# Independent scatters, a spread narrowing of two matrices, and a reordered first cycle in a filter, routing and expert kernel

## The chip, the core and the metric

The kernel runs on one core of a Trainium2 chip. Five engines work side by side: PE multiplies matrices (PEld loads its weights), ACT applies functions and casts, DVE and POOL do elementwise work, POOL also issues indirect DMAs, and SP issues the other DMAs. The metric is the device time of one execution in microseconds (us), the median of several.

## What is computed

Three layers in a row, all results in fp32:

```
X  = rfft(x, axis=1)                    # x: 4 x 3072 x 256
Y  = shrink(X @ (w_r + i w_i) + b)      # sign(.) * max(|.| - 0.01, 0), real and imaginary part
a  = irfft(Y).reshape(12288, 256)
e  = argmax(a @ w_gate); g = softmax weight of e
y  = g * (relu(a @ w1[e]) @ w2[e])      # 8 experts, the first 384 tokens of each; others give 0
h  = y @ w_in; out = (h * sigmoid(h)) @ w_out   # 256 -> 2048 -> 256
```

w_in and w_out arrive as float64.

## The kernel before

The Fourier transforms are products with tables (`first`, `s1`, `kphase`, `is2`, `third`). As 8 experts take 384 tokens each, only batch 0 and the first 1,024 tokens of batch 1 are computed (`near`); a branch at the end (L1269), on a flag that tells whether all experts are full, holds the rest and is not taken here. Tokens of a layer that no expert takes are zeros, written by `zero_out` on SP.

Every fp32 product is made of three matmuls (`mm3`, L205 to L207) on a high and a low part; `split` makes them, the high part by a cast on ACT (L189), the low part by a subtraction on DVE or POOL (L197). The float64 matrices are read as pairs of int32 and brought to fp32 by `narrow` (an absolute value on ACT, four operations on DVE, L868 to L874) and then split: `ffn_in` handles w_in in eight chunks, and forms on POOL the four sums s1 to s4 of its blocks (the `mixed` tensor); `ffn_out` handles w_out in eight chunks, a chunk at each of the steps that `AHEAD` names and at the first five steps of the first pair.

`experts` runs the order 0, 1, 2, E, 3, 4, E+1, 5, 6, E+2, 7, E+3. A number below E is one expert's own FFN (`first_ffn`: eight tiles hp of 128 x 384, rectified into hh on ACT and hl on DVE, which are consumed by the products y). E+q is the second FFN of a pair of experts (`second_ffn`): in each of eight cycles seven products h of a Winograd scheme, with the sums u (L1210) on DVE, Silu on ACT (L1151) and a split into gh and gl; m1 to m4, b2 and yT are the sums of the pair's inputs, made by `pair`. The three sums that come from `mixed` are loaded as mt and split into the tile ring, with the low part on POOL (`load`, `cut`). The products o with w_out of one cycle fill the next one; those of a pair's last cycle are closed in the first cycle of the next pair (`close`), evicted to the tile `tail` (L1182) and scattered to out by an indirect DMA of 128 rows (`scatter`, L1253). For the last pair the sums are finished at the end (L1241 to L1248), and the six scatters follow behind the branch (end of `body`). `gather` collects an expert's tokens by three indirect DMAs (L1040), `turn` transposes them (gtp) and, for expert 0, runs 12 matmuls on zeros behind (pw, L1063); `weights` loads an expert's weights as tiles st and splits them into w.

While experts 0 to 2 run, `beside` finishes the attention's second block and its routing: `third` (ps, ao, tp, lg, and lt, the transposed gate values, L602), `choose` (Exp on ACT), `route` (the counts bs, L695, and the tables tb, L753) and `slots`, which makes the positions of experts 3 to 7 with a temporary tmp of its own (L801).

A tile belongs to a ring of a few buffers (`bufs`), and its writer waits until the last reader of the buffer's earlier tile is done. The order on each engine is set by a list scheduler from the program's order and its dependencies; `after` adds an order between two instructions without a semaphore. Two scatters write the same tensor, so without more each waits for the one before.

Of the kernel before, what the change touches and what calls it, by code (L numbers as in the profile page):

```python
# [9 lines left out]
F32 = mybir.dt.float32  # L10
# [3 lines left out]
AF = mybir.ActivationFunctionType  # L14
# [9 lines left out]
P = 128  # L24
# [7 lines left out]
NF = 3  # L32
# [4 lines left out]
WARM = 11  # L37
AHEAD = 7, 15, 23
PMS = "vav"
# [114 lines left out]
class Kernel:  # L154
# [95 lines left out]
    def near(self):  # L250

        ads, self.bds, self.res = {}, {}, {}
        self.left = ExitStack()
        self.kp = self.left.enter_context(self.tc.tile_pool(name="kpa", bufs=2, reuse_waits="tile"))
        with self.stream("a", 3, "right"), self.sums("a", 2):
            self.warm()
            self.first()
            tables, spectra = self.load_tables(), self.kphase(0, ads)
            for g in (tables, spectra, tables, spectra, spectra):
                next(g)  # L260
            mix([tables, spectra, self.s1(1, ads), self.ffn_in()], [4, 10, 24, 15], lead=[0, 0, 0, 0])
            rest = self.kphase(1, ads, True)
            next(rest)
            with self.tc.issue_after(self.fetched):
                self.route_consts()
            mix([self.is2(0, (0, 1, 2), self.res)], [1])
            self.route(0, (0, 1, 2), self.res)
            self.rank()
            self.early = self.slots(self.cst, 0, EARLY, self.sel, "s")[0]
            for _ in rest:  # L270
                pass
# [271 lines left out]
    def choose(self, lt, out, gs):  # L543

        nc, v, bp = self.nc, self.nc.vector, self.bp
        oh, m2, sm = out
        sh = [P, lt.shape[1], gs.stop - gs.start, E]
        L = bp.tile(sh, F32, tag="L", name="L")
        mx = bp.tile(sh[:3] + [1], F32, tag="mx", name="mx")
        v.tensor_reduce(mx, lt, AX.X, ALU.max)  # L550
        sc = bp.tile(sh, F32, tag="sc", name="sc")
        v.tensor_tensor(sc, lt, mx.to_broadcast(sh), ALU.is_equal)
        v.tensor_tensor(L, lt, mx.to_broadcast(sh), ALU.subtract)
        nc.scalar.activation(L, L, AF.Exp)
        v.tensor_tensor(sc, sc, self.pri.to_broadcast(sh), ALU.mult)
        v.tensor_reduce(m2[:, :, gs], sc, AX.X, ALU.max)
        v.tensor_tensor(oh[:, :, :, gs].rearrange("p e b g -> p b g e"), sc, m2[:, :, gs].to_broadcast(sh), ALU.is_equal)
        v.tensor_reduce(sm[:, :, gs], L, AX.X, ALU.add)
# [230 lines left out]
    def slots(self, pool, s0, s1, sel, tag, work=None):  # L789
# [6 lines left out]
        if sel is None:  # L796
            v.tensor_copy(ent, T.rearrange("p x e -> p e x"))
        else:
            sh = [P, n, NF * SC, E]
            tmp = work.tile(sh, F32, name=f"tmp{tag}", bufs=1)  # L800
            v.tensor_tensor(tmp, T.rearrange("p (o x) e -> p o x e", o=1).to_broadcast(sh),  # L801
                            sel[:, s0:s1].rearrange("p s (o e) -> p s o e", o=1).to_broadcast(sh), ALU.mult)
            v.tensor_reduce(ent, tmp, AX.X, ALU.add)
# [81 lines left out]

    def ffn_in(self):

        W = 512
        nc, g = self.nc, self.nc.gpsimd
        for _ in range(LATE):  # L890
            yield
        for q in range(8):
            h, z = q % 2, (q // 2) * W
# [25 lines left out]
    def experts(self, again=False):  # L919
# [17 lines left out]
        def beside():  # L937

            with self.stream("b", 2, "left"):
                for n, _ in enumerate(self.third(1, self.res)):  # L940
                    yield 2 + 2 * n
                self.route(1, (0,), self.res)
                self.sl.extend(self.slots(self.mc, EARLY, E, self.sel, "t", self.bp)[0])
                self.filled()
            self.po, self.mb = pool("po", **ps), pool("mb")

        fw = self.ffn_out()
        if again:
            self.sl = self.compact(self.mc)
            self.po, self.mb = pool("po", **ps), pool("mb")  # L950
            side = iter(())
            for _ in self.ffn_in():
                pass
        else:
            self.sl = list(self.early)
            side = beside()
# [4 lines left out]
        xg = {e: self.gather(e) for e in order[:2]}  # L961
        xs[0] = self.turn(xg.pop(0), None if again else 12)
        ws = {e: self.weights(e, n) for e, n in zip(order[:2], (3, 4))}
# [3 lines left out]
        for at, ph in enumerate(order):  # L967
            if ph == E:
                for _ in side:
                    pass  # L970
                pre = self.pair()
            after = order[at + 1] if at + 1 < len(order) else E
            if after < E and after not in ws:
                xg[after] = self.gather(after)
                ws[after] = self.weights(after)
            part = self.first_ffn(ph, xs.pop(ph), ws[ph][0]) if ph < E else self.second_ffn(ph - E, pre)
            for m, _ in enumerate(part):
# [4 lines left out]
                while due is not None and due <= n:  # L982
                    due = next(side, None)
                if n in AHEAD or (ph == E and m < 5):
                    next(fw, None)
# [62 lines left out]
    def turn(self, rows, zeros=0, behind=None):  # L1048
# [11 lines left out]
        if zeros:  # L1060
            pw = self.pm.tile([P, 2 * D], F32, tag="y", name="pw")
            for n in range(zeros):
                self.after(self.nc.tensor.matmul(pw[:, :D], self.zr[:, :P], self.zr[:, :D], start=True, stop=True).ins, last.ins)  # L1063
        return xT

    def first_ffn(self, e, xT, ws):
# [5 lines left out]
        for j in range(NJ + 1):  # L1072
# [10 lines left out]
            if j > 0:  # L1083
                hh, hl = hs.pop(j - 1)
                for h in range(2):
                    w, c = w2[(j - 1) // 2], slice(h * P, (h + 1) * P)
                    self.mm3(yp[h], w[:, 0, (j - 1) % 2, c], w[:, 1, (j - 1) % 2, c], hh, hl, j == 1, j == NJ)
            yield
# [30 lines left out]
    def second_ffn(self, q, pre):  # L1119
# [58 lines left out]
        def close(us, s_):  # L1178
            for n, u in enumerate(us):
                second(u, s_, stop=n == len(us) - 1)  # L1180
            oo = rows(s_)
# [5 lines left out]
        load(1)  # L1187
        cut(0)
        for i in range(NI):
            load(i + 2)  # L1190
# [20 lines left out]

            for step in (1, 6, 0, 7, 4, 2, 0, 5, 3, 0) if final else (1, 0, 6, 2, 0, 7, 5, 0, 4, 3, 0):
                if step == 0:
# [5 lines left out]
                elif step == 2:  # L1219
                    add(u1, product(a12, b21), u1)  # L1220
                    self.unit[11] = gated(u1, "v", 2 * i, 0)
                elif step == 7:
                    add(u3, product(s3, m3), u2)
                elif step == 5:
# [3 lines left out]
                    add(u2, h, u2)  # L1228
                    self.unit[22] = gated(to, "p" if final else "v", 2 * i + 1, 1, "w0" if final else None)
                elif step == 4:  # L1230
# [21 lines left out]
    def scatter(self, oo, at, n):  # L1252
        self.nc.gpsimd.indirect_dma_start(  # L1253
            out=self.o["out"][0:n], out_offset=bass.IndirectOffsetOnAxis(ap=at, axis=0),
            in_=oo, in_offset=None, bounds_check=n - 1, oob_is_err=False)

# [47 lines left out]
```

## Time and profile before

| | us |
|---|---|
| median of 3 runs | 657.82 |
| lowest, highest | 654.78, 659.46 |
| the profiled execution | 659.92 |
| its span, first to last instruction | 658.1 |
| PE busy in it | 608.9 |

The rows further down come from that one profiled execution. Times count from the start of its span; L12 is line 12 of the kernel before. "out<-in" names the tiles an instruction writes and reads; what stands behind "<-" in brackets is what ended an engine's idle time.

### The profile page before, as it was taken

How to read it: one execution, taken by the hardware profiler on the slowest of the kernel's cores; microseconds unless marked ns; L12 is line 12 of the kernel's file. 1: busy time of each engine (PE TensorE's matmuls, PEld its weight loads, DVE VectorE, ACT ScalarE, POOL GpSimd, SP SyncE). 2: the span in 40 equal slices, each digit the busy share in tenths (PEclk: the TensorE clock that was granted, in tenths of full speed). 3: DMA queues.
4: the chain of work that ended last, by engine and by line, in shares of the span. 5: the costliest groups of instructions: out<-in, count | busy, mean ns of one | idle time of the engine just before them, and what ended most of it. 6: DMA issues, size and time to landing. Idle time of an engine off the chain costs nothing. (4 is left out here: it accounts for less than half of the span.)

```text
span 658.1 us, 11494 instructions
## 1 busy us (share of the span) xinstructions
PE 608.9 (93%) x4128; PEld 562.8 (86%) x4128; DVE 424.4 (64%) x832; ACT 339.7 (52%) x721; POOL 198.3 (30%) x201
## 2 busy tenths in 40 slices
PE   9999979999979989899999999999999999899940
PEld 8988769568967779799889999999999999799940
DVE  2447796355953659889987785577785574665630
ACT  2545554344533544566565675555665564565520
POOL 1004461000060001356663423453213443354312
PEclk9999999999998999879999999999999999999985
DMA  8547985965266766532434442323432300110000
GB/s 219 164 143 229 325 255 157 233 174 163 105 218 194 189 194 187 188 90 96 135 93 132 151 143 90 121 79 118 136 109 89 121 25 29 37 32 14 1 21 32
DMA packets 66010, 86.08 MB, mean 131 GB/s; under 512 B 6068, under 2 KB 55864, under 8 KB 65944
## 3 DMA queue, kind: packets, MB, share of 16 engines
q1 hardware_dynamic: 53976, 69.53, 34.9%
q10 hardware_dynamic: 9664, 9.44, 4.7%
q0 software_dynamic: 2304, 6.29, 2.9%
q8 instruction: 34, 0.56, 0.4%
q14 instruction: 32, 0.26, 0.2%
HBM read 54.31 MB, written 30.93 MB: 130 GB/s over the span
## 5 line engine op out<-in xcount | busy, mean ns | idle before, releaser
L1210 DVE TENSOR_TENSOR u<-h,u 128x384 f32<-128x384 f32 x224 | 117.3, 552 | 57.5 <-PE h L207 51.0
L1151 ACT ACTIVATE u<-u 128x384 f32<-128x384 f32 x128 | 64.6, 522 | 73.8 <-DVE u L1210 72.0
L206 PE MATMUL o<-wo,gl 128*128 128x256 f32 x369 | 100.2, 283 | 0.8 <-POOL gl L197 0.8
L207 PE MATMUL o<-wo,gh 128*128 128x256 f32 x369 | 99.9, 283 | 0.0
L205 PE MATMUL o<-wo,gh 128*128 128x256 f32 x369 | 87.3, 283 | 0.1
L197 POOL TENSOR_TENSOR gl<-u,gh 128x384 fp32r<-128x384 f32 x62 | 66.8, 1094 | 31.8 <-ACT gh L189 25.5
L197 POOL TENSOR_TENSOR ring<-mt,ring 128x384 fp32r<-128x384 f32 x32 | 37.5, 1173 | 119.9 <-ACT ring L189 118.3
L206 PEld LDWEIGHTS o<-wo,gl 128*128 128x128 f32 x369 | 70.0, 190 | 1.5 <-POOL gl L197 1.4
L207 PEld LDWEIGHTS o<-wo,gh 128*128 128x128 f32 x369 | 70.2, 190 | 0.0
L205 PEld LDWEIGHTS o<-wo,gh 128*128 128x128 f32 x369 | 65.6, 191 | 0.4 <-ACT gh L189 0.4
L189 ACT CAST gh<-u 128x384 fp32r<-128x384 f32 x126 | 63.6, 510 | 4.1 <-PE o L207 2.1
L197 DVE TENSOR_TENSOR w<-st,w 128x512 fp32r<-128x512 f32 x64 | 43.7, 694 | 25.2 <-ACT w L189 19.9
L1081 DVE SCALAR_TENSOR_TENSOR hl<-hp,hh 128x384 fp32r<-128x384 f32 x64 | 35.1, 553 | 36.1 <-ACT hh L1080 30.1
L205 PE MATMUL yp<-wri,xk 128*128 128x256 f32 x188 | 57.4, 305 | 0.4 <-ACT xk L454 0.4
L206 PE MATMUL yp<-wri,xk 128*128 128x256 f32 x188 | 54.8, 291 | 0.3 <-DVE xk L453 0.3
L207 PE MATMUL yp<-wri,xk 128*128 128x256 f32 x188 | 54.0, 287 | 0.0
L189 ACT CAST w<-st 128x512 fp32r<-128x512 f32 x64 | 38.8, 621 | 26.0 <-DMA st<-in_moe_w 15.8
L1080 ACT ACTIVATE hh<-hp 128x384 fp32r<-128x384 f32 x64 | 31.1, 490 | 37.2 <-PE hp L207 23.1
L205 PE MATMUL y<-hh,w 128*128 128x384 f32 x128 | 44.3, 346 | 3.2 <-ACT hh L1080 3.2
L205 PE MATMUL hp<-xT,w 128*128 128x384 f32 x128 | 44.2, 346 | 2.5 <-ACT w L189 2.5
L206 PE MATMUL hp<-xT,w 128*128 128x384 f32 x128 | 43.8, 343 | 0.1
L207 PE MATMUL hp<-xT,w 128*128 128x384 f32 x128 | 43.5, 341 | 0.0
(254 smaller groups left out, 1508.8 us busy)
## 6 DMA issues: line engine op xcount, KB each, us to landing
st<-in_moe_w SPq DMA_DIRECT2D x64, 256.0 KB
out<-zt SPq DMA_DIRECT2D x48, 256.0 KB
b_d<-bo ACTq DMA_DIRECT2D x12, 512.0 KB
mt<-mixed SPq DMA_DIRECT2D x32, 192.0 KB
xt<-in_x SPq DMA_DIRECT2D x15, 384.0 KB
nt<-in_moe_w_in SPq DMA_DIRECT2D x8, 512.0 KB
nt<-in_moe_w_out SPq DMA_DIRECT2D x16, 256.0 KB
a_d<-ao SPq DMA_DIRECT2D x8, 384.0 KB
```

The source lines that it names most:

```text
L189: self.lastact = self.nc.scalar.copy(dst, src)
L197: return e.tensor_tensor(dst, src, raw(hi), ALU.subtract).ins
L205: first = nc.tensor.matmul(out, lh, rh, start=start, stop=False)
L206: nc.tensor.matmul(out, ll, rh, start=False, stop=False)
L207: return first.ins, nc.tensor.matmul(out, lh, rl, start=False, stop=stop).ins
L1080: self.rectified = nc.scalar.activation(hh, hp, AF.Relu).ins
L1081: self.evicted = nc.vector.scalar_tensor_tensor(hl, hp, 0.0, raw(hh), ALU.max, ALU.subtract).ins
L1151: act.activation(sg, sg, AF.Silu)
L1210: v.tensor_tensor(to, h, u, ALU.add)
```

## The change

- `scatter` declares all scatters of a pass independent of one another (the rows of one expert's tokens are its own).
- `second_ffn` yields once after load(0), load(1) and cut(0), so that these come ahead of the next expert's gathers and weights.
- `AHEAD` names five steps instead of three, and the first pair's steps narrow three chunks instead of five.
- `ffn_in` takes a range of chunks: four run where eight did, four beside `is2`; its sums go from POOL to DVE.
- A tiny Silu follows the last Exp of the routing, so that ACT's table is loaded there.
- The temporary of the second `slots` takes a buffer of the ring "hh" that holds rectified tiles.
- The zeros behind expert 0's transposes are 6 on the F32 zero tile, not 12 on its FR copy, which POOL writes.
- In the first cycle of pairs 1 to 3 the fill comes earlier, with a tile u5; in the last pair the first closing product comes after expert 7's last y.
- The last cycle's unit 22 has its low part on DVE.

```diff
-AHEAD = 7, 15, 23
+AHEAD = 4, 8, 12, 16, 20
...
-            mix([tables, spectra, self.s1(1, ads), self.ffn_in()], [4, 10, 24, 15], lead=[0, 0, 0, 0])
+            mix([tables, spectra, self.s1(1, ads), self.ffn_in(0, 4)], [4, 10, 24, 10], lead=[0, 0, 0, 0])
...
-            mix([self.is2(0, (0, 1, 2), self.res)], [1])
+            mix([self.is2(0, (0, 1, 2), self.res), self.ffn_in(4, 8)], [10, 7])
...
-        nc.scalar.activation(L, L, AF.Exp)
+        self.exps = nc.scalar.activation(L, L, AF.Exp).ins
...
-            tmp = work.tile(sh, F32, name=f"tmp{tag}", bufs=1)
+            tmp = (work.tile(sh, F32, name=f"tmp{tag}", bufs=1) if tag == "s" else
+                   self.mh.tile([P, CAP], F32, tag="hh", name="tmp")[:, :n * NF * SC * E].rearrange("p (s x e) -> p s x e", s=n, e=E))
...
-        nc, g = self.nc, self.nc.gpsimd
+        nc, g = self.nc, self.nc.vector
...
+                tiny = self.mc.tile([P, 1], F32, name="tiny")
+                self.after(self.nc.scalar.activation(tiny, self.zt[:, 0, :1], AF.Silu).ins, self.exps)
                 self.route(1, (0,), self.res)
-                self.sl.extend(self.slots(self.mc, EARLY, E, self.sel, "t", self.bp)[0])
+                self.sl.extend(self.slots(self.mc, EARLY, E, self.sel, "t")[0])
...
-        xs[0] = self.turn(xg.pop(0), None if again else 12)
+        xs[0] = self.turn(xg.pop(0), None if again else 6)
...
+            part = self.first_ffn(ph, xs.pop(ph), ws[ph][0]) if ph < E else self.second_ffn(ph - E, pre)
+            if ph >= E:
+                next(part)
             after = order[at + 1] if at + 1 < len(order) else E
...
-                if n in AHEAD or (ph == E and m < 5):
+                if n in AHEAD or (ph == E and m < 3):
...
-                self.after(self.nc.tensor.matmul(pw[:, :D], self.zr[:, :P], self.zr[:, :D], start=True, stop=True).ins, last.ins)
+                self.after(self.nc.tensor.matmul(pw[:, :D], self.zt[:, 0, :P], self.zt[:, 0], start=True, stop=True).ins, last.ins)
...
-                second(u, s_, stop=n == len(us) - 1)
+                first = second(u, s_, stop=n == len(us) - 1)[0]
+                if end and not n:
+                    self.after(first, self.lasty)
...
         cut(0)
+        yield
...
+            early = q and not i
+            if final:
+                steps = 1, 6, 0, 7, 4, 2, 0, 5, 3, 0
+            elif early:
+                steps = 1, 0, 2, 0, 6, 7, 5, 0, 4, 3
+            else:
+                steps = 1, 0, 6, 2, 0, 7, 5, 0, 4, 3, 0
...
-                    add(u1, product(a12, b21), u1)
-                    self.unit[11] = gated(u1, "v", 2 * i, 0)
+                    to = mh.tile([P, CAP], F32, tag="hl", name="u5") if early else u1
+                    add(to, product(a12, b21), u1)
+                    self.unit[11] = gated(to, "v", 2 * i, 0)
...
-                    self.unit[22] = gated(to, "p" if final else "v", 2 * i + 1, 1, "w0" if final else None)
+                    self.unit[22] = gated(to, "v", 2 * i + 1, 1, "w0" if final else None)
...
-        self.nc.gpsimd.indirect_dma_start(
+        ins = self.nc.gpsimd.indirect_dma_start(
...
+        group = f"rows{n}"
+        self.tc.declare_no_dep(ins, group=group, reason="a token has one place of one expert")
+        self.tc.add_to_no_dep_group(group, ins)
```

What the change does to the order is shown at three places. The first is the end of POOL's order: gw is the low part of unit 22, the rows with oo stand inside the branch that is not taken, those with tail behind it. Before:

```order
L197 TENSOR_TENSOR gl<-u_15533,gh 128x384 [waits Activation_49]
L197 TENSOR_TENSOR gw<-u_15630,gw 128x384 [waits DVE_49,Activation_49]
L1253 DMA out<-oo,dstc 12288x256 [waits DMASW3_49,DVE_49]
...
L1269 UNCONDITIONAL_BRANCH
...
L1253 DMA out<-tail,dstt 4096x256 [waits DMASW4_49,DMASW3_49,DMASW5_49,DMASW2_49,DMASW6_49,DMASW1_49,DMASW7_49,DMASW0_49,DVE_49]
L1253 DMA out<-tail,dstt 4096x256 [waits DMASW2_49,DVE_49]
```

After:

```order
L197 TENSOR_TENSOR gl<-u_15536,gh 128x384 [waits Activation_49,Pool_49]
L197 TENSOR_TENSOR gl<-u_15535,gh 128x384 [waits Activation_49]
L1269 DMA out<-oo,dstc 12288x256 [waits DMASW4_49,DVE_49,Activation_49]
...
L1288 UNCONDITIONAL_BRANCH
...
L1269 DMA out<-tail,dstt 4096x256 [waits DMASW3_49,DMASW4_49,DMASW2_49,DMASW5_49,DMASW1_49,DMASW6_49,DMASW0_49,DMASW7_49,DVE_49,Activation_49]
L1269 DMA out<-tail,dstt 4096x256 [waits DVE_49,Activation_49]
```

POOL's split gw is gone from ahead of the branch, and the second scatter of tail waits for no DMA (DMASW) any more.

The second is PE while expert 1 runs, from shortly before the last lt (gate values) of the second routing; y and hp are expert products, bs and tb belong to the routing. Before, where bs and tb come 45 and 126 rows behind lt:

```order
L205 MATMUL y_2647<-hh,w_2493 128x384
L206 MATMUL y_2647<-hh,w_2493 128x384
L602 MATMUL lt<-ident,ls 128x128 [waits Activation_49]
L207 MATMUL y_2646<-hl,w_2493 128x384 [waits DVE_49]
L207 MATMUL y_2647<-hl,w_2493 128x384
L1058 MATMUL gtp<-ident,xg 128x128 [waits DVE_49]
L1058 MATMUL gtp<-ident,xg 128x128
L1058 MATMUL gtp<-ident,xg 128x128 [waits DVE_49]
L1058 MATMUL gtp<-ident,xg 128x128
L205 MATMUL y_2646<-hh,w_2548 128x384 [waits Activation_49]
L206 MATMUL y_2646<-hh,w_2548 128x384
L205 MATMUL y_2647<-hh,w_2548 128x384
```

After:

```order
L589 MATMUL tp<-ident,ao_2453 128x128 x3
L597 MATMUL lg<-aT,wg 32x128 [waits DVE_49]
L597 MATMUL lg<-aT,wg 32x128 x3
L602 MATMUL lt<-ident,ls 128x128 [waits Activation_49]
L695 MATMUL bs<-inc,rt 128x8 [waits DVE_49,PE_49]
L698 MATMUL bs<-inc,rt 128x8
L753 MATMUL tb<-ft,pm 128x72 [waits DVE_49,PE_49]
L753 MATMUL tb<-ft,pm 128x72 x7
L1212 MATMUL o_3245<-zr 128x512 [waits PE_49,Pool_49]
L1212 MATMUL o_3246<-zr 128x512
L1212 MATMUL o_3247<-zr 128x512 [waits DVE_49]
L205 MATMUL y_2652<-hh,w_2330 128x384 [waits Activation_49]
```

Before, the matmuls of experts stand between lt, bs and tb; now bs and tb follow lt directly, and the experts' y with the third rectified tile comes behind them.

The third is POOL before the first pair's first cycle: wo is a low part of w_out, ring one of the pair's mixed sums, xg with srct the gathers of expert 3. Before:

```order
L197 TENSOR_TENSOR wo<-na,wo 128x512 [waits Activation_49]
L1040 DMA xg<-attn_71,srct 128x256 [waits DMAHW3_49,DMAHW2_49,DMAHW4_49,DMAHW1_49,DMAHW5_49,DMAHW0_49,DMAHW6_49,DMASW1_49,DMAHW7_49,DVE_49,PE_49]
L1040 DMA xg<-attn_71,srct 128x256 [waits DMASW2_49]
L1040 DMA xg<-attn_71,srct 128x256 [waits DMASW3_49]
L197 TENSOR_TENSOR ring<-mt,ring 128x384 [waits DMAHW7_49,PE_49,Activation_49]
L197 TENSOR_TENSOR ring<-mt,ring 128x384 [waits DMAHW1_49,Activation_49]
L197 TENSOR_TENSOR ring<-mt,ring 128x384 [waits DMAHW6_49,Activation_49,Pool_49]
```

After:

```order
L197 TENSOR_TENSOR wo<-na,wo 128x512 [waits Activation_49] x2
L197 TENSOR_TENSOR ring<-mt,ring 128x384 [waits PE_49,DMAHW3_49,Activation_49,Pool_49]
L197 TENSOR_TENSOR ring<-mt,ring 128x384 [waits DMAHW6_49,Activation_49]
L197 TENSOR_TENSOR wo<-na,wo 128x512 [waits Activation_49]
L1045 DMA xg<-attn_71,srct 128x256 [waits DMAHW4_49,DMAHW2_49,DMAHW5_49,DMAHW1_49,DMAHW7_49,DMAHW0_49,DMASW1_49]
L1045 DMA xg<-attn_71,srct 128x256 [waits DMASW2_49]
L1045 DMA xg<-attn_71,srct 128x256 [waits DMASW3_49]
L197 TENSOR_TENSOR ring<-mt,ring 128x384 [waits DMAHW2_49,Activation_49,Pool_49]
```

Two of the three ring splits now stand ahead of expert 3's gathers.

## Rows read from the trace of the kernel before

**Rows 1.** The page: slices of the span, PE busy and its granted clock

```profile
PE   9999979999979989899999999999999999899940
...
PEclk9999999999998999879999999999999999999985
```

**Rows 2.** Stretches: busy us and (instructions) per engine, clock, DMA share

```profile
core 0: us, PE busy (x) PEld busy (x) DVE busy (x) ACT busy (x) POOL busy (x), PEclk, DMA share, GB/s
...
50.00:100.00 50.00, 45.54 (x296) 37.76 (x295) 41.78 (x62) 28.14 (x60) 26.80 (x28) 1.00 0.84 265
100.00:150.00 50.00, 49.91 (x398) 36.00 (x397) 23.79 (x58) 19.87 (x41) 0.99 (x1) 1.00 0.69 190
...
287.40:350.00 62.60, 59.99 (x420) 58.16 (x420) 57.47 (x90) 38.32 (x83) 38.11 (x32) 1.00 0.36 113
350.00:450.00 100.00, 100.00 (x671) 99.61 (x670) 69.19 (x128) 61.50 (x132) 39.39 (x37) 1.00 0.37 118
```

**Rows 3.** The chain that ended last, from 634 us on

```profile
634.29 4.48 DMA out<-tail,dstt
...
639.55 2.43 DMA out<-tail,dstt
...
652.07 1.20 POOLq L1300
```

**Rows 4.** Timeline of POOL from 618 us: start, length, instruction, [idle before]

```profile
621.37 2.00 POOL L197 TENSOR_TENSOR gl<-u,gh 128x384 fp32r<-128x384 f32 x2 [5.71 <-ACT gh L189]
628.61 1.02 POOL L197 TENSOR_TENSOR gw<-u,gw 128x384 fp32r<-128x384 f32 x1 [5.23 <-ACT gw L189]
634.29 1.00 POOL L1253 DMA_INDIRECT out<-tail,dstt  x1 [4.66 <-DVE tail L1248]
...
652.29 0.98 POOL L1253 DMA_INDIRECT out<-tail,dstt  x1 [2.20 <-DMA out<-tail,dstt]
```

**Rows 5.** Timeline of DVE from 629 us to the end

```profile
629.74 1.09 DVE L1248 TENSOR_TENSOR tail<-h,tail 128x256 f32<-128x256 f32 x3 [1.27 <-ACT u L1151]
...
632.53 1.09 DVE L1248 TENSOR_TENSOR tail<-h,tail 128x256 f32<-128x256 f32 x3 [1.24 <-PE h L207]
```

**Rows 6.** Timeline of POOL from 275 us: expert 3's gathers, ring splits

```profile
275.64 1.49 POOL L1040 DMA_INDIRECT xg<-attn,srct  x1 [7.14 <-DMA st<-in_moe_w]
...
279.77 1.96 POOL L197 TENSOR_TENSOR ring<-mt,ring 128x384 fp32r<-128x384 f32 x2
```

**Rows 7.** Timeline of PE at expert 0 and at the second routing

```profile
197.55 0.61 PE L205 MATMUL hp<-xT,w 128*128 128x384 f32 x2 [2.48 <-ACT w L189]
...
201.38 1.89 PE L1063 MATMUL pw<-zr 128*128 128x256 f32 x12
...
246.05 0.27 PE L602 MATMUL lt<-ident,ls 128*128 128x128 f32 x1
...
270.43 1.08 PE L753 MATMUL tb<-ft,pm 128*128 128x72 f32 x8
...
280.82 0.69 PE L206 MATMUL h<-m,ring 128*128 128x384 f32 x1 [1.37 <-POOL ring L197]
```

**Rows 8.** Stretches between 198 and 288 us, columns as in rows 2

```profile
198.60:202.00 3.40, 3.40 (x13) 3.40 (x12) 0.69 (x2) 0.00 (x0) 0.00 (x0) 0.50 0.65 191
202.00:245.30 43.30, 40.28 (x243) 30.59 (x241) 23.52 (x48) 19.04 (x40) 1.29 (x1) 1.00 0.68 198
...
249.80:273.70 23.90, 22.29 (x127) 21.10 (x126) 23.41 (x65) 13.36 (x28) 3.33 (x4) 1.00 0.66 205
273.70:287.40 13.70, 10.82 (x31) 9.30 (x32) 9.14 (x23) 7.79 (x17) 6.67 (x7) 0.50 0.30 90
```

**Rows 9.** Timeline of DVE from 250 us, inside the second routing

```profile
250.35 0.18 DVE L552 TENSOR_TENSOR sc<-lt,mx 128x32 f32<-128x32 f32 x1
...
269.17 1.21 DVE L741 TENSOR_TENSOR pm<-iota,r 128x1024 fp32r<-128x1024 f32 x1
```

**Rows 10.** Waits of PE: us in total, times, longest

```profile
PE h L205 <- ACT m L189: 3.0, 2, 2.0
```

More of the change, by code (lines that the diff above doesn't have):

```diff
@@ L884, in ffn_part, with ffn_in @@
         return a
-    def ffn_in(self):
+    def ffn_in(self, q0, q1):
         W = 512
-        nc, g = self.nc, self.nc.gpsimd
+        nc, g = self.nc, self.nc.vector
         for _ in range(LATE):
             yield
-        for q in range(8):
+        for q in range(q0, q1):
             h, z = q % 2, (q // 2) * W
@@ L951, in experts @@
             side = iter(())
-            for _ in self.ffn_in():
+            for _ in self.ffn_in(0, 8):
                 pass
@@ L975, in experts @@
                 ws[after] = self.weights(after)
-            part = self.first_ffn(ph, xs.pop(ph), ws[ph][0]) if ph < E else self.second_ffn(ph - E, pre)
             for m, _ in enumerate(part):
@@ L1086, in first_ffn @@
                     w, c = w2[(j - 1) // 2], slice(h * P, (h + 1) * P)
-                    self.mm3(yp[h], w[:, 0, (j - 1) % 2, c], w[:, 1, (j - 1) % 2, c], hh, hl, j == 1, j == NJ)
+                    self.lasty = self.mm3(yp[h], w[:, 0, (j - 1) % 2, c], w[:, 1, (j - 1) % 2, c], hh, hl, j == 1, j == NJ)[1]
             yield
@@ L1210, in add @@
                 v.tensor_tensor(to, h, u, ALU.add)
-            for step in (1, 6, 0, 7, 4, 2, 0, 5, 3, 0) if final else (1, 0, 6, 2, 0, 7, 5, 0, 4, 3, 0):
+            early = q and not i
[5 more added lines that the diff above has]
+                steps = 1, 0, 6, 2, 0, 7, 5, 0, 4, 3, 0
+            for step in steps:
                 if step == 0:
@@ L1252, in scatter @@
     def scatter(self, oo, at, n):
-        self.nc.gpsimd.indirect_dma_start(
+        ins = self.nc.gpsimd.indirect_dma_start(
             out=self.o["out"][0:n], out_offset=bass.IndirectOffsetOnAxis(ap=at, axis=0),
-            in_=oo, in_offset=None, bounds_check=n - 1, oob_is_err=False)
+            in_=oo, in_offset=None, bounds_check=n - 1, oob_is_err=False).ins
+        group = f"rows{n}"
+        self.tc.declare_no_dep(ins, group=group, reason="a token has one place of one expert")
+        self.tc.add_to_no_dep_group(group, ins)
 @with_exitstack
```

## Prediction

> **What bounds the kernel now.** I first read the page's slices and then the table of stretches, to see whether one engine sets the pace and where it doesn't. PE is at nine tenths or more in most slices, and its granted clock is full but for a dip in the middle and the end [rows 1]; from 350 to 450 us PE is busy for all of 100.00 us [rows 2]. There no other engine's work can shorten anything. Time can only come from places where PE stands still or runs at the lower level, and there are four: 50 to 100 us, the middle (184 to 287 us), 287 to 350 us, one wait at the start of the last pair, and the tail after PE's last matmul.
>
> The tail is read next, in the chain that ended last and in the timelines of POOL and DVE. The last sums into the tail tile end at 632.53 + 1.09 = 633.62 [rows 5]. What follows is only six scatters: the first is issued at 634.29, and each of the others waits for the landing of the one before, so that the sixth stands at 652.29 [rows 3, 4]. From the second, whose DMA starts at 639.55, to the sixth that is 12.74 us for four, 3.19 each, of which the DMA is 2.43. The sixth lands about 2.4 later, near 654.7, and the span ends 3.4 after that.
>
> Then the middle. After the last step of the attention's second block PE stands at a low clock for 13.70 us, in which it has only 10.82 us of work at 0.50; before that DVE is busy for 23.41 of 23.90 us [rows 8]. DVE was late there, I take it, because the second routing, the splits of expert weights and the narrowing share it.
>
> **The change part by part.**
>
> *Scatters declared independent, and the final unit 22 split on DVE.* POOL's last work of its own before the flag's load and the branch is one split at 628.61, 1.02 long, and the first scatter stands 4.66 after it [rows 4], which is 0.67 after the last sum. In the changed order that split is no longer in front of them on POOL (first order above), so POOL is free from 621.37 + 2.00 = 623.37. With the same 4.66 it reaches the scatters at 628.0 and then waits for data: three tiles are summed by 629.74 + 1.09 = 630.83, three by 633.62 [rows 5]. Six issues without waits follow one another as gathers do on the same queue: three gathers stand between 275.64 and 279.77 [rows 6], 1.38 each. From 631.0 that gives the sixth at 631.0 + 5 x 1.38 = 637.9, its landing at 640.3 and the span's end, with the same 3.4, at 643.7: minus 14.4. DVE takes one more split among its last sums, which I put at 0.4, so minus 14.0. Bounds: were the first scatter still at 634.29 with its 4.48 [rows 3], the sixth would be issued at 641.2 and, if it too takes 4.48, land at 645.7; minus 9. With 1.30 for an issue and no delay on DVE, minus 15.5. Mid-kernel scatters lose their waits too, but PE is full there [rows 2], and POOL is idle for more than half of it; I cost them at nothing, and a later POOL result would be the loss if that cover were gone.
>
> One rule speaks against the main term. The Trainium skill ("DMA: Bandwidth & Descriptors", section "SWDGE vs HWDGE vs iDMA") says that only one queue is allocated for the DMAs that GpSimd issues. If that one queue worked off one DMA at a time, six scatters would still go one after another. The gathers at 275.64, on that queue, show issues 1.38 apart without the DMA's 2.43 in between [rows 3, 6], so the trace leans to overlap, though for gathers, which read scattered rows, and not for scatters, which write them. By the rule the tail would be the second rival below.
>
> *The middle.* Three edits meet here: the 12 zero matmuls become 6 from a tile that needs no wait and stand elsewhere, the temporary of the second routing takes a place in the ring of the experts' rectified tiles, and W sums are split ahead of gathers.
> (a) The 12 matmuls of 1.89 us run after the 2.48 us wait at 197.55 and at half clock [rows 7, 8]; the six now stand in front of it, inside the wait. That removes 1.89, and perhaps the lower clock of 198.60 to 202.00 (3.40 us at 0.50, 1.7 lost): minus 1.9 to minus 3.6, I take minus 3.
> (b) In before, PE carries 116 matmuls of experts between the second transposed gate (lt, 246.05) and the tables of the routing (tb, 270.43) [rows 7]. In the changed order there are none (second order above): expert 1's third rectified tile must wait until the temporary is read. So PE idles for the length of the routing's chain. It took 24.4 us, stretched by other work on DVE that is busy 98% [rows 8]; that is the upper bound. The lower: some thirty small DVE instructions of 0.1 to 0.3 us, by the 0.18 of one such row, and the larger ones up to 1.21 [rows 9], with Exp, bs and tb between, some 10 us. I take 12, nearer to the low end because the changed DVE order has only one weight split in that chain. 46 matmuls of experts that stood ahead of lt are now behind it too; if PE set the pace there (40.28 of 43.30 busy [rows 8]) lt comes up to 46 x 0.176 = 8.1 us earlier (127 matmuls in 22.29 us give 0.176 each [rows 8]), and if DMA did (0.68 there) not at all; I take 4. After tb come 156 matmuls of experts, 27.5 us, and the lower clock behind such a hole I put at 3 us, between the 1.7 lost after 198.60 and the 5.4 lost after 273.70 [rows 8].
> (c) What goes in return: pair 0 ran from 273.70 to 287.40 on 31 matmuls which at full clock are 31 x 0.176 = 5.5 us, so 8.2 us of those 13.70 go to idling and the low clock [rows 8], because its operands were split late on DVE and its ring tiles behind three gathers on POOL (from 275.64; PE waits for ring until 280.82 [rows 6, 7]). Now two ring splits stand ahead of the gathers (third order above), and DVE's routing is over some 20 us before.
> Sum: before reaches the end of those 31 matmuls at 287.4. After: lt at 246.05 less 4 less 3 of (a), 239; tb done at 251; 156 matmuls to 278.5; low clock 281.5; 31 matmuls 287.0. Without the low clock it is 284.0; I take the middle, 285.4: minus 2. Ends: lt at 235, a chain of 10 and no low clock give 278, minus 9; lt not moved, a chain of 14 and 4 us of low clock give 297, plus 10.
>
> *The other places.* The last pair: close no longer stands ahead of m casts on ACT. PE waited 2.0 at the longest for m [rows 10]; I take all of it, bounds 0 and minus 2.0. From 287.40 to 350 PE lacks 62.60 - 59.99 = 2.61 while DVE is busy 57.47 [rows 2]; two narrowed chunks of w_out are done before instead of in it. Minus 1.5, bounds 0 and minus 2.6. From 50 to 100 PE lacks 4.46 with DMA at 0.84 [rows 2]; half of w_in's loads move behind it, into a stretch where PE lacks 0.09 and DVE is busy only 23.79 of 50 [rows 2], which hides the sums that go from POOL to DVE. Minus 2, bounds plus 1 (DVE busier at its 41.78) and minus 4.4. The table load for Silu (1.3 us on ACT) moves from the start of pair 0 into the hole; it is in the term above.
>
> **Sum.** -14 - 2 - 2 - 1.5 - 2 = -21.5 on the profiled execution's 659.92 gives 638.4. That run stands 2.1 above the median of 657.82; scaled to it, 636.4, and I say 637.
>
> **Rivals.**
> 1. *The tail alone gains.* The middle's hole costs more than I take and eats the small gains: -14 + 7.5 - 2 is about 651 on the profiled time, 649 on the median. For it: nothing fills PE in the hole, and DVE was full before. Against: the same work of DVE remains, only earlier.
> 2. *Scatters still drain one by one.* 2.43 each after a first of 4.48 from 631.4: landing 648.0, end 651.4, tail -6.7 instead of -14: 644.
> 3. *Slower.* The hole is as long as before's whole 24.4, as expert 1's next weights are loaded behind four loads of w_out, and PE's clock stays at 0.50 through the 27.5 us of expert matmuls after it: (24.4 - 12) + (27.5 - 3) on my middle's -2 is +35, less 19.5 elsewhere: 675 on the profiled time, 673 on the median. It decides once the middle costs over 26 (1% slower). For it: half clock followed each of the waits of rows 8. Against: it lasted 3.40 and 13.70, the latter with more waits inside.
> 4. *No hole.* lt comes early since PE set the pace, and clock stays full: middle -9: 659.9 - 28.5, 629 on the median.
> 5. *The declaration does nothing*, the scatters wait as before: about 650.
>
> **How the numbers follow.** Forecast .60 (628 to 646), rival 1 .14, rival 2 .10, rival 4 .08, rival 5 .04, rival 3 .04. A measurement of this kernel can tell about 1%, 6.6 us, so faster means under 651.2. All of the forecast, 2, 4 and most of 1 and 5 lie there: .91 faster; .05 within; .04 slower. The range takes in the forecast, rivals 2 and 4 and half of rival 1: 624 to 650.
>
> **What would show it.** Right: six scatters some 1.4 us apart, the first near 631 and the span's end 10 us or so after PE's last matmul; no wait for m or ring at pair 0; a hole of 10 to 14 us in PE ahead of tb, with a lower clock behind it; 12 zeros gone from behind the wait. Wrong: scatters 2.4 or more apart (rival 2), tb not ahead of expert matmuls in time, a clock of 0.50 for over 15 us, or new waits of PE in 100 to 184 for DVE.

## The result, and the profile after

The changed kernel takes 632.93 us (median of 4 runs, 631.7 to 633.7), the kernel before 656.9 beside it: a ratio of 0.963, 95% interval 0.959 to 0.967. 637 with a range of 624 to 650 was predicted. The profiled execution took 633.7 with a span of 631.9, 26.2 less than before.

The page's slices of PE and its clock, as in [rows 1], and stretches with the columns of [rows 2]:

```profile
PE   9999998999989967999999999999999999999993
...
PEclk9999999999999986999999999999999999999997
```

```profile
50.00:100.00 50.00, 49.35 (x334) 42.28 (x333) 36.27 (x64) 27.20 (x58) 5.85 (x6) 1.00 0.75 239
100.00:150.00 50.00, 47.47 (x389) 33.49 (x387) 32.46 (x79) 22.45 (x46) 9.23 (x6) 1.00 0.80 226
225.00:232.40 7.40, 5.40 (x39) 2.86 (x35) 4.28 (x12) 3.40 (x7) 0.00 (x0) 0.90 0.86 291
232.40:242.70 10.30, 3.06 (x14) 2.80 (x13) 6.43 (x30) 2.61 (x5) 0.46 (x2) 0.50 0.27 88
242.70:250.00 7.30, 7.30 (x28) 6.98 (x28) 6.64 (x20) 2.71 (x5) 1.22 (x1) 0.63 0.12 30
...
281.70:358.10 76.40, 76.40 (x537) 76.36 (x536) 58.93 (x105) 48.40 (x105) 41.56 (x38) 1.00 0.35 109
```

The dip in the middle is still there, shorter and ahead of the first pair. From 281.7 to 358.1, the first pair, PE and its weight loads (the second number) fill all of 76.40 us; in the kernel before the same work had 78.49 and 76.63 of 81.10 us (the row stands with a4 below).

POOL and DVE at the end, as in [rows 4, 5]:

```profile
609.55 2.00 POOL L197 TENSOR_TENSOR gl<-u,gh 128x384 fp32r<-128x384 f32 x2 [5.70 <-ACT gh L189]
619.07 1.20 POOL L1269 DMA_INDIRECT out<-tail,dstt  x1 [7.52 <-DVE tail L1264]
620.57 0.98 POOL L1269 DMA_INDIRECT out<-tail,dstt  x1 [0.30 <-issue]
...
625.73 0.98 POOL L1269 DMA_INDIRECT out<-tail,dstt  x1 [0.30 <-issue]
```

```profile
617.84 1.09 DVE L1264 TENSOR_TENSOR tail<-h,tail 128x256 f32<-128x256 f32 x3 [0.55 <-PE h L207]
...
620.69 1.08 DVE L1264 TENSOR_TENSOR tail<-h,tail 128x256 f32<-128x256 f32 x3 [1.30 <-PE h L207]
```

No split stands between gl at 609.55 and the scatters; the first starts at 619.07, when the first three sums end (617.84 + 1.09 = 618.93), and the sixth 6.66 us later instead of 18.00. PE's last matmul ends at 621.1.

PE from expert 0 to the first pair, as in [rows 7]:

```profile
192.83 2.75 PE L1068 MATMUL pw<-zt 128*128 128x256 f32 x12
...
195.23 0.52 PE L205 MATMUL y<-hh,w 128*128 128x384 f32 x1
...
232.15 0.47 PE L602 MATMUL lt<-ident,ls 128*128 128x128 f32 x1 [0.36 <-ACT ls L600]
234.26 0.57 PE L695 MATMUL bs<-inc,rt 128*128 128x8 f32 x2 [1.63 <-DVE inc L691]
...
240.86 1.89 PE L753 MATMUL tb<-ft,pm 128*128 128x72 f32 x8 [5.61 <-DVE pm L741]
...
281.74 0.51 PE L205 MATMUL o<-wo,gh 128*128 128x256 f32 x3
```

The trace has twelve records (x12) for the six matmuls on zeros. lt comes at 232.15 instead of 246.05, tb 8.7 us behind it instead of 24.4, and between them PE waits 5.61 for pm and 1.63 for inc: the stretch 232.40 to 242.70 has 3.06 us of PE at 0.50, the one behind it a clock of 0.63.

Cut at five marks that every run has, the time lies as follows (us, from the timelines of PE in one profiled execution of each kernel; "yp" is the end of the attention's last yp, "o" the first product with w_out in the first pair, "zeros" the zeros of the second pair, "hp" expert 6's first hp, "PE end" the last matmul; from the zeros to hp it is 177.6 to 177.9 in every run; the changed kernel's o stands three matmuls, some 0.5 us, earlier in PE's order; below, labels are shortened to b1, a2 and so on). One of a4's four executions, of 647.1 us, fell in a slower state and is left out of its median.

Each ratio is to the kernel before, timed beside the run (medians of 655.8 to 657.2):

| kernel | median | ratio to before, 95% | to yp | yp to o | o to zeros | hp to PE end | PE end to span's end |
|---|---|---|---|---|---|---|---|
| before | 656.9 | | 186.7 | 98.9 | 81.0 | 88.7 | 25.1 |
| after | 632.9 | .959 to .967 | 184.2 | 97.5 | 76.3 | 85.4 | 10.8 |
| b1_free_scatter | 646.7 | .976 to .990 | 187.4 | 96.9 | 79.8 | 88.7 | 13.9 |
| b2_free_scatter_dve | 642.4 | .969 to .984 | 186.7 | 96.1 | 81.0 | 88.7 | 10.5 |
| a1_scatter_wait | 646.0 | .974 to .988 | 185.8 | 96.8 | 76.6 | 86.0 | 22.3 |
| a2_tmp_own | 629.4 | .950 to .964 | 185.1 | 91.3 | 75.9 | 85.5 | 10.9 |
| d2_tmp_sg | 626.9 | .950 to .957 | 186.1 | 90.7 | 76.0 | 85.5 | 10.9 |
| c3_both | 631.1 | .960 to .967 | 184.8 | 90.5 | 79.0 | 85.5 | 10.9 |
| a4_old_ahead | 636.6 | .966 to .976 | 185.3 | 94.8 | 80.7 | 85.4 | 10.8 |
| a5_win_whole | 635.4 | .966 to .973 | 183.2 | 99.6 | 76.3 | 85.4 | 10.8 |
| a10_pool_sums | 632.4 | .959 to .966 | 184.1 | 96.0 | 76.3 | 85.4 | 10.5 |
| a6_close_free | 635.9 | .966 to .971 | 184.5 | 96.6 | 76.6 | 87.9 | 10.5 |
| a7_old_steps | 632.8 | .959 to .967 | 185.0 | 95.0 | 76.6 | 86.1 | 10.5 |
| a3_no_zeros | 635.1 | .961 to .969 | 185.1 | 97.9 | 76.5 | 85.4 | 10.8 |

So 26.2 splits into 14.3 (tail), 4.7 (o to zeros), 3.3 (last pair), 2.5 (to yp) and 1.4 (yp to o). The columns "to yp" and "yp to o" vary by 2 or 3 us between runs that don't differ there; the other three by half a microsecond, but for b1's 79.8. So the 1.4 can't be told from none: yp to o is 97.3 on the mean of the three runs that go on from before, and 96.8 on that of the eight that have the changed kernel's temporary. The intervals of b1, b2 and a1 lie below 1 but take in 0.98, so that a gain of 2% is neither shown nor excluded for them; what these runs say is read from the columns.

### The profile page after: what moved, and what is told of

The parts are those of the page before. It is cut to its first block, busy times and chain, and to the rows that moved or that the text cites. A ratio compares the mean times of both kernels' runs of the same rounds, so it can differ in the third digit from the quotient of the medians.

```text
span 631.9 us, 11495 instructions
## 1 busy us (share of the span) xinstructions
PE 601.5 (95%) x4128; PEld 561.4 (89%) x4128; DVE 420.5 (67%) x849; ACT 340.3 (54%) x722; POOL 185.5 (29%) x184
## 4 chain that ended last, share of the span: by engine, by line
PE 86%; DMA 5%; DVE 3%; issue 2%; ACT 2%; POOL 1%; SPq 0%; POOLq 0%; ACTq 0%; DVEq 0%
PE o L206 7%; PE o L207 7%; PE o L205 7%; PE h L205 6%; PE h L207 6%; PE h L206 6%; PE xp L436 3%; PE y L205 3%; PE y L207 3%; PE hp L205 3%; PE hp L206 3%; PE hp L207 3%; PE yp L205 3%; PE y L206 3%; PE yp L207 3%; PE yp L206 3%
## 5 line engine op out<-in xcount | busy, mean ns | idle before, releaser
L197 POOL TENSOR_TENSOR ring<-mt,ring 128x384 fp32r<-128x384 f32 x32 | 38.9, 1216 | 134.9 <-ACT ring L189 129.3
L197 POOL TENSOR_TENSOR gl<-u,gh 128x384 fp32r<-128x384 f32 x62 | 64.5, 1059 | 28.0 <-ACT gh L189 27.3
L205 PE MATMUL yp<-wri,xk 128*128 128x256 f32 x188 | 56.1, 298 | 1.4 <-DVE tail L476 1.4
L1086 DVE SCALAR_TENSOR_TENSOR hl<-hp,hh 128x384 fp32r<-128x384 f32 x64 | 35.2, 553 | 29.2 <-ACT hh L1085 24.4
L206 PE MATMUL yp<-wri,xk 128*128 128x256 f32 x188 | 53.9, 287 | 0.0
L207 PE MATMUL yp<-wri,xk 128*128 128x256 f32 x188 | 53.8, 286 | 0.0
L189 ACT CAST w<-st 128x512 fp32r<-128x512 f32 x64 | 38.9, 621 | 22.3 <-DMA st<-in_moe_w 11.8
L205 PE MATMUL y<-hh,w 128*128 128x384 f32 x128 | 44.3, 346 | 1.0 <-ACT hh L1085 1.0
L205 PE MATMUL hp<-xT,w 128*128 128x384 f32 x128 | 43.6, 340 | 0.0
L206 PE MATMUL hp<-xT,w 128*128 128x384 f32 x128 | 43.3, 338 | 0.0
L206 PE MATMUL y<-hh,w 128*128 128x384 f32 x128 | 43.2, 338 | 0.0
```

What stands on the lines that cost most here:

```text
L189: self.lastact = self.nc.scalar.copy(dst, src)
L197: return e.tensor_tensor(dst, src, raw(hi), ALU.subtract).ins
L205: first = nc.tensor.matmul(out, lh, rh, start=start, stop=False)
L206: nc.tensor.matmul(out, ll, rh, start=False, stop=False)
L207: return first.ins, nc.tensor.matmul(out, lh, rl, start=False, stop=stop).ins
L1086: self.evicted = nc.vector.scalar_tensor_tensor(hl, hp, 0.0, raw(hh), ALU.max, ALU.subtract).ins
```

## The experiments

**The tail.** b1_free_scatter is the kernel before with the declaration of the scatters, b2_free_scatter_dve that and unit 22's low part on DVE (the first pair of lines), a1_scatter_wait the changed kernel without the declaration.

```diff
-                    self.unit[22] = gated(to, "p" if final else "v", 2 * i + 1, 1, "w0" if final else None)
+                    self.unit[22] = gated(to, "v", 2 * i + 1, 1, "w0" if final else None)
...
-        self.nc.gpsimd.indirect_dma_start(
+        ins = self.nc.gpsimd.indirect_dma_start(
...
-            in_=oo, in_offset=None, bounds_check=n - 1, oob_is_err=False)
+            in_=oo, in_offset=None, bounds_check=n - 1, oob_is_err=False).ins
+        group = f"rows{n}"
+        self.tc.declare_no_dep(ins, group=group, reason="a token has one place of one expert")
+        self.tc.add_to_no_dep_group(group, ins)
```

> The kernel before with one edit: the scatters of a pass are declared independent. Theory (the tail's gain is the waits between scatters): the first final scatter still stands 1.3 us behind PE's last matmul, because POOL's split gw is ahead of the branch; the six then follow at 1.3 us instead of 5.3 and 3.2, so the last is issued 6.7 instead of 18.0 us after the first: 11.3 us less, about 646. Rival A (the move of unit 22 to DVE makes the tail): at most 3 us less, about 654. Rival B (scatters in mid-kernel matter too): over 14 us less, with PE's idle time between 287 and 600 us gone.

> As b1_free_scatter, and unit 22's low part of the last cycle on DVE. Theory: POOL is at the scatters when the first three tiles are summed, so the first stands about 2 us ahead of PE's last matmul instead of 1.3 behind: 3.4 us less than b1_free_scatter, 14.5 less than before, about 643. Rival A: the same end, but b1_free_scatter gives little of it. Rival C (POOL's branch path is late for another reason, such as code that is fetched): no difference from b1_free_scatter.

> The changed kernel without the declaration, so that each scatter waits for the one before. Theory: the span between the first and the last issue goes from 6.7 back to 18 us: 11 us more than the changed kernel, about 644, with PE's last matmul where it was (about 621). Rival B: PE's last matmul comes later too, as POOL's splits stand behind waiting scatters in mid-kernel.

POOL at the end of b1_free_scatter, b2_free_scatter_dve and a1_scatter_wait:

```profile
626.10 1.02 POOL L197 TENSOR_TENSOR gw<-u,gw 128x384 fp32r<-128x384 f32 x1 [5.24 <-ACT gw L189]
632.07 1.00 POOL L1253 DMA_INDIRECT out<-tail,dstt  x1 [4.95 <-DVE tail L1248]
633.37 0.99 POOL L1253 DMA_INDIRECT out<-tail,dstt  x1 [0.30 <-issue]
...
638.52 0.98 POOL L1253 DMA_INDIRECT out<-tail,dstt  x1 [0.30 <-issue]
```

```profile
618.64 2.01 POOL L197 TENSOR_TENSOR gl<-u,gh 128x384 fp32r<-128x384 f32 x2 [5.71 <-ACT gh L189]
628.17 1.20 POOL L1253 DMA_INDIRECT out<-tail,dstt  x1 [7.53 <-DVE tail L1248]
...
634.84 0.98 POOL L1253 DMA_INDIRECT out<-tail,dstt  x1 [0.30 <-issue]
```

```profile
620.87 1.19 POOL L1269 DMA_INDIRECT out<-tail,dstt  x1 [7.54 <-DVE tail L1264]
626.44 0.98 POOL L1269 DMA_INDIRECT out<-tail,dstt  x1 [4.38 <-DVEq L1285]
629.82 0.98 POOL L1269 DMA_INDIRECT out<-tail,dstt  x1 [2.40 <-DMA out<-tail,dstt]
...
639.39 0.98 POOL L1269 DMA_INDIRECT out<-tail,dstt  x1 [2.20 <-DMA out<-tail,dstt]
```

b1's tail is 13.9 against 25.1: 11.2 for the declaration alone, as expected (646.7 by the median, 646 was put), with the scatters 1.29 apart behind gw and a gap of 4.95. b2 has no gw there, the first scatter starts 2.1 us ahead of PE's end instead of 1.6 behind it (PE's ends are 630.2 and 630.5), and the tail is 3.4 shorter again; rivals A and C fall. What fills the 4.95 us behind gw is not split further here; that time lies under other work once gw is gone. a1's scatters are 5.6 and then 3.4 to 3.2 apart, and its tail is 11.5 longer; PE ended at 622.9 against 621.1, of which 1.6 stand ahead of yp, so rival B has nothing for it. In b1 and b2 the stretch from the zeros to hp is 177.7 as before: free scatters in mid-kernel are worth nothing there, as full PE said.

**The hole.** a2_tmp_own gives the temporary a tile of its own again; d2_tmp_sg puts it in the ring sg, in which the pair's sums tm and u3 lie.

```diff
-            tmp = (work.tile(sh, F32, name=f"tmp{tag}", bufs=1) if tag == "s" else
-                   self.mh.tile([P, CAP], F32, tag="hh", name="tmp")[:, :n * NF * SC * E].rearrange("p (s x e) -> p s x e", s=n, e=E))
+            tmp = work.tile(sh, F32, name=f"tmp{tag}", bufs=1)
...
-                self.sl.extend(self.slots(self.mc, EARLY, E, self.sel, "t")[0])
+                self.sl.extend(self.slots(self.mc, EARLY, E, self.sel, "t", self.bp)[0])
```

```diff
-                   self.mh.tile([P, CAP], F32, tag="hh", name="tmp")[:, :n * NF * SC * E].rearrange("p (s x e) -> p s x e", s=n, e=E))
+                   self.mg.tile([P, CAP], F32, tag="sg", name="tmp")[:, :n * NF * SC * E].rearrange("p (s x e) -> p s x e", s=n, e=E))
```

> The changed kernel with the routing's temporary in a tile of its own, as before. The order then has experts' matmuls again between lt, bs and tb, and no ring split ahead of expert 3's gathers. Theory (the hole is the price of an early routing that pair 0 gets back): no idle time of 5 us ahead of tb, but pair 0 stalls again as before, 3 us idle and over 10 us at half clock near 265 to 280; in sum 1 to 5 us slower than the changed kernel, 634 to 638. Rival (the hole is a plain loss, by the 9.2 us that PE idles in 225 to 242.7 and some 4 that the low clock costs up to 250): 8 to 13 us faster, 620 to 625.

> The changed kernel with the routing's temporary in the ring of the pair's sums (sg) instead of that of the rectified tiles (hh). In its order experts' matmuls stand between lt and tb, and two ring splits ahead of expert 3's gathers. Theory (the hole comes from the ring hh alone; what a2_tmp_own still lost at the first pair came from the memory that its temporary held until the routing's end): no hole, from the attention's last yp to the first pair's first o 86 to 91 us (97.5 in the changed kernel, 91.3 in a2_tmp_own), 623 to 629. Rival (the pair's sums tm now wait for the temporary, so that m is late instead): 92 to 97 us there, 630 to 634.

PE in a2_tmp_own and in d2_tmp_sg, from lt or tb to the first pair:

```profile
240.15 0.27 PE L602 MATMUL lt<-ident,ls 128*128 128x128 f32 x1
...
262.13 1.08 PE L753 MATMUL tb<-ft,pm 128*128 128x72 f32 x8 [0.16 <-DVE pm L741]
...
267.69 0.69 PE L207 MATMUL h<-m,wi 128*128 128x384 f32 x1 [2.20 <-DVE m L197]
...
272.30 0.69 PE L206 MATMUL h<-m,ring 128*128 128x384 f32 x1 [1.36 <-POOL ring L197]
...
276.40 0.52 PE L205 MATMUL o<-wo,gh 128*128 128x256 f32 x3
```

```profile
262.99 0.98 PE L753 MATMUL tb<-ft,pm 128*128 128x72 f32 x8
...
269.98 0.44 PE L205 MATMUL h<-m,wi 128*128 128x384 f32 x1 [3.82 <-ACT m L189]
...
271.21 0.69 PE L207 MATMUL h<-m,ring 128*128 128x384 f32 x1 [0.26 <-DVE m L197]
```

What the ring hh does in the changed kernel shows on ACT, which writes the rectified tiles; entt is the last reader of the temporary:

```profile
244.83 0.49 ACT L1085 ACTIVATE hh<-hp 128x384 fp32r<-128x384 f32 x1 [8.98 <-DVE entt L804]
```

ACT waits 8.98 us until the temporary is read, and the experts' y that need this tile stand behind tb on PE. For a2 both expectations missed: the hole goes and the first pair's stall comes back (2.20 for m, 1.36 for ring), as theory said, but the run gains 3.6 us by the medians and 6.2 from yp to o. Hole and stall were not an even exchange. d2 has 90.7 from yp to o, within what theory expected, and 626.9 is the shortest of all: 6 us below the changed kernel, with intervals that don't meet. So the ring hh cost the changed kernel 3.6 us by a2's median and 6 by d2's. Two things in d2's expectation are not shown. The memory that a2's temporary held makes no difference that can be told: yp to o is 91.3 in a2 and 90.7 in d2. And the wait of 3.82 at 269.98 is not the rival's: it is for an m cast from yf, which lies in no buffer of sg, and in d2's trace no engine's wait is put down to the temporary.

c3_both tried for what a2 has left; its edits against a2 are:

```diff
-AHEAD = 4, 8, 12, 16, 20
+AHEAD = 4, 8, 12
...
-                if n in AHEAD or (ph == E and m < 3):
+                if n in AHEAD or (ph == E and m < 5):
...
                 self.after(ins.ins, self.narrowed)
+                if s == EARLY:
+                    self.after(ins.ins, self.cutlow)
...
-                self.split("ap", t[:, 0], t[:, 1], ring[i])
+                self.cutlow = self.split("ap", t[:, 0], t[:, 1], ring[i])
```

> The kernel of a2_tmp_own with two further edits: expert 3's gathers are ordered behind the first split of the first pair's ring, and the chunks of w_out are narrowed at steps 4, 8, 12 and the first five of the first pair. Theory (what is left at the first pair's start in a2_tmp_own, a wait of 2.2 us for m on DVE, one of 1.4 for ring on POOL, and the low clock behind them, comes from DVE's load and from POOL's queue): both waits go, 4 to 8 us faster than a2_tmp_own, 621 to 625. Rival (the two chunks cost in the first pair what they save ahead of it): 628 to 632.

Its rival held, with 631.1: yp to o fell by 0.8 and o to zeros rose by 3.1, with stalls of PE again:

```profile
276.00:354.00 78.00, 76.20 (x524) 74.30 (x523) 66.09 (x108) 49.53 (x106) 44.71 (x39) 1.00 0.38 117
```

**The narrowing.** a4_old_ahead has the old steps in the changed kernel:

```diff
-AHEAD = 4, 8, 12, 16, 20
+AHEAD = 7, 15, 23
...
-                if n in AHEAD or (ph == E and m < 3):
+                if n in AHEAD or (ph == E and m < 5):
```

> The changed kernel with the chunks of w_out narrowed at the old steps (three ahead of the first pair, five in it). Theory (those two chunks made the first pair's DVE the limit): from the first pair's first o to the zeros of the second pair it takes 79 to 81 us again instead of 76.3, PE's weight-load column falls short of PE's, and the run is 3 to 5 us slower than the changed kernel, 636 to 638. Rival (the splits of W ahead of gathers or the early table load freed that stretch): 76 us there, 632 to 634.

The first pair, o to zeros, in a4_old_ahead and then in the kernel before:

```profile
280.00:360.80 80.80, 78.33 (x537) 76.19 (x536) 68.81 (x113) 50.70 (x109) 46.07 (x41) 1.00 0.39 123
```

```profile
285.50:366.60 81.10, 78.49 (x533) 76.63 (x533) 68.68 (x110) 50.00 (x107) 46.09 (x40) 0.99 0.36 113
```

The two read alike: DVE busy for 68.81 and 68.68 us, weight loads 76.19 and 76.63, against 58.93 and 76.36 in the changed kernel, which needs no longer than its weight loads. a4 gives back 4.4 of the 4.7 us, as theory expected, and what is left is within what the column varies by; no part of the splits ahead of gathers or of the table load shows in it.

**The start.** a5_win_whole runs all of w_in in the first mix, its sums still on DVE; a10_pool_sums has w_in in two parts and the sums on POOL (the last pair of lines).

```diff
-            mix([tables, spectra, self.s1(1, ads), self.ffn_in(0, 4)], [4, 10, 24, 10], lead=[0, 0, 0, 0])
+            mix([tables, spectra, self.s1(1, ads), self.ffn_in(0, 8)], [4, 10, 24, 15], lead=[0, 0, 0, 0])
...
-            mix([self.is2(0, (0, 1, 2), self.res), self.ffn_in(4, 8)], [10, 7])
+            mix([self.is2(0, (0, 1, 2), self.res)], [1])
...
-        nc, g = self.nc, self.nc.vector
+        nc, g = self.nc, self.nc.gpsimd
```

> The changed kernel with all eight chunks of w_in in the first mix, as before, their sums still on DVE. Theory: PE's busy time from 50 to 100 us falls from 49.35 to about 45.5, and that from 100 to 150 rises from 47.47 to about 49.9; the attention's last yp comes 1.5 to 2.5 us later, and so does the end: 634 to 636. Rival (DVE, which has the sums now, becomes late there): 4 us and more, with waits of PE on DVE ahead of 100 us. Rival (that split gives nothing): 632 to 633.

> The changed kernel with the sums of w_in's blocks on POOL again. Theory (POOL's sums and the splits behind them held up what the first 100 us wait for): the attention's last yp, 183.2 to 185.8 us with the sums on DVE, comes at 186 to 187.5 as before, and the run is 1.5 to 3 us slower, 634.5 to 636. Rival (neither the sums nor the split of w_in matter; PE's gain there is from the order that the scheduler finds): 183 to 186, 632 to 634.

a5_win_whole, with the columns of [rows 2]:

```profile
50.00:100.00 50.00, 47.39 (x315) 40.13 (x314) 44.44 (x80) 28.95 (x63) 12.20 (x12) 1.00 0.82 265
100.00:150.00 50.00, 50.00 (x414) 35.98 (x413) 25.05 (x64) 20.21 (x41) 0.00 (x0) 1.00 0.72 201
```

PE's work moves between the two stretches in the direction expected (47.39 from 50 to 100 us, where 45.5 was put), but yp comes at 183.2, not later; with the sums on POOL it comes at 184.1, as a10's rival had it. Neither edit alone carries the 2.1 us by which yp is earlier on the mean (184.8 in the eleven runs that go on from the changed kernel, 186.9 in the three that go on from before). POOL's busy time from 50 to 100 us was 26.80 [rows 2], and is 5.85 in the changed kernel, 12.20 in a5 and 11.39 in a10; that either edit frees POOL enough would fit, but both undone at once was not tried. Why a5's median is 2.5 higher stays open; its o comes 1.1 later, within what that column varies by. That the median lies in theory's 634 to 636 is no proof of its reason.

**The last pair.** a6_close_free takes the order of the closing product away, a7_old_steps the new order of steps.

```diff
-                if end and not n:
-                    self.after(first, self.lasty)
...
-            early = q and not i
+            early = False
```

> The changed kernel without the order of the last pair's first closing product behind expert 7's last y. Theory (the closing products and their evictions stood ahead of the m casts on ACT): from expert 6's first hp to PE's last matmul it takes 88.7 us as before instead of 85.4, with a wait of h for an m of some 2 us; 635 to 637. Rival (the reordered steps of a pair's first cycle gave it): 85.4 us, 632 to 634.

> The changed kernel with the old order of steps in the first cycle of pairs 1 to 3. Theory (PE is full in pairs 1 and 2, and in the last pair a6_close_free left 0.8 of the 3.3 us unexplained): 177.7 us from the second pair's zeros to expert 6's first hp as in every run so far, and 86 instead of 85.4 us from there to PE's last matmul: 633 to 634. Rival (the order does more of the last pair than that): 87 to 88 us, 635 to 636.

a6's last pair takes 87.9, a7's 86.1, against 85.4: the closing order is worth 2.5 of the 3.3. The 0.7 of the steps, which theory put, can hardly be told from none, as a1 with the new steps has 86.0. The wait for m of [rows 10] is back in a6, at half its length:

```profile
PE h L205 <- ACT m L189: 1.0, 1, 1.0
```

The rest of a6's 2.5 doesn't show as a wait but in PE's weight loads, which fill 84.97 of its 87.9 us and 85.10 of 85.4 in the changed kernel.

**The zeros.** a3_no_zeros has no matmuls on zeros behind expert 0's transposes.

```diff
-        xs[0] = self.turn(xg.pop(0), None if again else 6)
+        xs[0] = self.turn(xg.pop(0), None if again else 0)
```

> The changed kernel without the six matmuls on zeros behind expert 0's transposes; nothing that they compute is used. Theory (they lie in a wait for expert 0's next weights and cost nothing; they keep the clock up): the matmul behind them stays where it is, and the granted clock falls to 0.50 for some us near 196 to 202: 0 to 2 us slower, 633 to 635. Rival (they are on the path): up to 2.7 us faster, 630 to 632.

```profile
190.00:202.00 12.00, 10.88 (x57) 9.24 (x57) 6.67 (x13) 5.75 (x12) 3.62 (x4) 1.00 0.83 252
```

```profile
194.15 0.44 PE L205 MATMUL y<-hh,w 128*128 128x384 f32 x1 [0.40 <-issue]
```

The clock stays at 1.00 from 190 to 202 without them, so they don't keep it up. The matmul behind them does not stay where it is: it stands 9.0 us behind yp (194.15), and 11.0 in the changed kernel (195.23). So the zeros are on PE's path there, and the six took 2.75 us where the twelve before took 1.89 [rows 7]. But the 2.0 us don't reach the end. lt stands 50.3 us behind yp in a3 and 47.9 in the changed kernel, and the run isn't faster: 635.1, which can't be told from 632.9. The wait of 2.48 and the low clock of [rows 7, 8] are gone in a3 too, so the six zeros are not what took them away; what did is not settled.

The first yield of `second_ffn` and the tiny Silu were not undone by themselves.

## Why the prediction was right, and where its steps were off

The time was right because its largest term was. That the middle came out near its figure is luck, and the other three terms were too small by 5.0 us together.

- *Scatters and unit 22*: -14 was put, -14.3 measured, and both halves as reasoned: 11.2 for the waits, 3.4 for POOL's way to the branch. The extra 0.4 for DVE was not seen. Rivals 2 and 5 fell: issues 1.29 apart on one queue, without the landing of 2.43 in between. The Trainium skill's one queue ("DMA: Bandwidth & Descriptors", section "SWDGE vs HWDGE vs iDMA") is no contradiction to that: it gives the number of queues and not that one queue works off one DMA at a time, which the prediction supposed for rival 2. Scatters in it overlap here, as the gathers did.
- *Middle*: -2 was put, -1.4 measured, which can't be told from none, from parts that were off and cancelled. lt came 13.9 us earlier (7 was put; 2.5 of the 13.9 are the earlier yp), and the chain was about as put (tb ends 10.6 behind lt, 12 was put). From tb's end to o it took 39.0 us: 196 matmuls, which at the 0.176 of [rows 8] would be 34.5 by my estimate, with 5.05 us of that time at a clock of 0.50 and 1.8 us idle; 156 matmuls, 3 for the clock and up to 31 more, 36.0 in all, were put. What step (c) said of the return held (no wait for m or ring at pair 0), and rival 1's "nothing fills PE in the hole" too, but not the thought that the hole is the price of that return: a2 and d2 have no hole, stall at pair 0, and are 3.6 and 6 us ahead. Step (a) put -3 on the zeros, and that step failed: they take longer than before, and in a3, which has none, the low clock of [rows 8] is gone too.
- *287 to 350*: -1.5 was put, -4.7 measured. The cause was right (a4). The size was taken from PE's idle time, 2.61. The same row of [rows 2] had weight loads of 58.16 in 62.60, a lack of 4.44, and about that came back: PE's column counted 78.33 us as busy in a4 and 76.40 in the changed kernel for the same 537 matmuls, while the weight loads were 76.19 and 76.36.
- *Last pair*: -2.0 was put, with that as bound, -3.3 measured, 2.5 of it by the closing order. The bound failed as the term before did: only PE's wait was counted, not the time beside it in which weight loads were lacking (2.9 us in a6, 0.3 in the changed kernel).
- *Start*: -2 was put, -2.5 measured (2.1 on the mean of the runs), and the reason, the loads of w_in, is not borne out: a5 moves them back, and its yp is no later. Its median is 2.5 us higher, so that the question isn't closed; what made the gain stays open.
- Rivals 1, 3 and 4: the smaller terms gained 11.9 us, and the middle lost none; the low clock is seen only between 225 and 250, and at the last matmuls; and the hole was there.

## What to carry to other kernels

Where a tail is a row of DMAs that wait for one another only because they write one tensor, count one issue each instead of one landing each, and look at what stands ahead of the first on its queue. A temporary that is put into another stage's ring of buffers makes that stage wait for it: choose the ring whose owner is idle then. Where PE's column and that of its weight loads differ in a stretch that is otherwise full, look at the lack of the second: in the first pair it was 4.4 us and 4.7 were won, in a6's last pair 2.9, of which the closing order is worth 2.5.

## What had not been expected

The granted clock stayed at 1.00 from 190 to 202 us in runs with and without the zeros there. In the first pair DVE's load showed in the weight loads more than in PE's waits: with DVE busy for 68.8 of 80.8 us (a4) the pair took 4.4 us longer, of which PE's waits name 2.5; with 58.9 of 76.4 PE waited for nothing.
